# Another hand-written order for the opening's steps, with fewer and smaller filler products, and alternating state buffers

## The chip, the cores and the metric

The kernel runs on one core of one Trainium2 chip. The metric is the device time of one execution in microseconds (us). TensorE does the matrix products (PE in the profile, its weight loads PEld), VectorE is DVE, ScalarE is ACT, GpSimd is POOL, and SyncE (SP) issues nearly all loads.

## The reference

A recurrent attention with a decaying state feeds a gated feed-forward layer. There are 4 batches, 8 heads, 768 time steps and heads of 48; the layer has 3072 tokens, 384 inputs and 1536 hidden units, all float32.

```python
for t in range(S):
    cur = np.einsum('bhd,bhe->bhde', u[None] * kt, vt)
    y[:, :, t] = np.einsum('bhd,bhde->bhe', rt, state + cur)
    state = wt[:, :, :, None] * state + np.einsum('bhd,bhe->bhde', kt, vt)
...
gate = 1.0 / (1.0 + np.exp(-(x @ w_gate)))
val = x @ w_val
return (gate * val @ w_out).astype(np.float32)
```

## The kernel before

Time is cut into six chunks of 128 steps. A chunk of one batch is a block q (24 of them, four to a chunk, numbered chunk by chunk). The hidden units are cut into 12 slices f of 128, each with its own weights. The opening covers the blocks 0 to 11 and prepares 12 and 13. It runs the layer for the blocks 0 and 1 (group 0), 2 and 3 (group 1) and 4 to 7 (group 2), while the weights are still being loaded and split. After it a regular loop takes chunk after chunk; that loop is the same in both kernels.

The opening is not scheduled by a compiler. `ORDER` is a text of some 620 words; each word is one step, and the steps are issued exactly in that order. Every engine takes its own instructions in the order in which they were issued, so a word's place decides what it stands behind on each engine that it uses. The queue of SP is such an order too. Semaphores hold back an instruction whose input is not there, and everything behind it on its engine waits along.

The words that the text below uses, with q the block, g the group, f the slice:

- `pinq`, `tokq`, `wordsf`: loads on SP (decay, k and r of a block, L341; its r, v, k by token, L346; the raw weights of a slice, L279). `pin` and `tok` have two buffers each, so a load waits for the last reader of the block two before it.
- `pkq`: DVE scan of the decays (L396), a reciprocal (L400) and k times the decays (L402). `prq`: the second scan (L413) and r times it (L418). `fadeq`: the state times the chunk's decay (L408).
- `tkq`: PE transposes k (L428); `kTq`: ACT copies it out (L432). `guardq`: ACT sums squares for a bounds check (L423).
- `ssq`: PE scores and state sums (L447, L550). `m0q`, `m1q`: DVE masks the scores (L538). `midq`, `keepq`: the state at mid-chunk (ACT L559 for q below 4, else DVE L561) and at the end (DVE L565). `sxq`: PE products of state, scores and values (L461, L574).
- `b1_q` to `b4_q`: the bonus term (POOL L366, L369, DVE L373, POOL L386 and L387). `ybq`: PE adds it (L582); `y0q`, `y1q` take the result out (ACT L587 for q below 4, else DVE L590). `txq`: PE transposes it (L596); `xfq`, `xhq`, `xlq` copy it and split it (ACT L609, ACT L616 or L618, DVE L622).
- `wgf`, `wbf`, `wtf`: float64 weights become float32 (ACT L286, DVE L297, DVE L301). `whf`, `wlf`: their high and low parts (ACT L324, DVE L327).
- `pgg_f`, `pug_f`: PE products with gate and value weights (L632 for the first few slices, in plain float32 with one product; L635 else, three products with the parts). `sg`, `hm`, `hh`, `hl`: sigmoid (ACT L646), gate times value (DVE L653), its high part (ACT L660), its low part (DVE L664). `dng_f`: PE products with the output weights (L675 plain, L679 in three parts).
- `first`, `st256`, `st512`: PE products of constants, 256 or 512 columns wide (L741). Nothing reads their result; the text calls them unread products.

The functions that the diff touches beside the table:

Of the kernel before, what the change touches and what calls it, by code (L numbers as in the profile page):

```python
# [37 lines left out]
ORDER = """
first pin0 pk0 pin1 pr0 tk0 st512 tok0 kT0 ub guard0 pk1 tok1 ss0 st256 words4 pr1 tk1 st512 m00 b1_1 m10 kT1 words0 b1_0 mid0
ss1 keep0 b2_0 wg4 b2_1 b3_0 words1 sx0 st512 st512 mid1 wb4 b4_0 b3_1 wg0 wt4 yb0 pin2 b4_1 m01 m11 keep1 y00 wb0 wh4 sx1 wt0  # L40
guard1 yb1 wl4 words5 y10 tx0 y01 y11 wb1 wg1 tx1 st512 pk2 xf1 xf0 pin3 pg0_0 pr2 tok2 tk2 sg0_0 pu0_0 wt1 guard2 tok3 kT2 pk3
pg0_1 words2 ss2 sg0_1 b1_2 hm0_0 pu0_1 mid2 m02 b2_2 wg5 keep2 words3 b1_3 b3_2 dn0_0 m12 pr3 tk3 sx2 words6 kT3 wg2 b2_3 hm0_1
ss3 xh0 wb2 b4_2 b3_3 dn0_1 pin4 mid3 m03 guard3 keep3 b4_3 m13 wg3 sx3 wt2 tok4 wb3 yb2 words7 wb5 pg0_2 y02 wt3 xh1 wh2 pu0_2
wt5 sg0_2 pin5 pk4 pg0_3 wh5 yb3 tok5 hm0_2 tk4 xl1 y03 pu0_3 y13 pr4 kT4 sg0_3 dn0_2 xl0 fade4 hm0_3 pg0_4 guard4 wl5 pu0_4
sg0_4 pk5 wg6 ss4 y12 wg7 tx2 wb6 tx3 pg0_5 mid4 b1_5 keep4 hm0_4 m04 dn0_3 b2_5 sg0_5 m14 xf2 xf3 pr5 wh1 pu0_5 tk5 sx4 b1_4
kT5 xh2 wt6 ss5 pin6 b2_4 hm0_5 wh6 pg1_0 m05 fade5 hh0_4 wl6 wh3 pu1_0 words8 sg1_0 hl0_4 hh0_5 xl2 dn0_4 wb7 m15 pg0_6 hm1_0
b3_4 wl2 pu0_6 sg0_6 guard5 pg1_1 b4_4 hm0_6 mid5 hh0_6 hl0_5 xh3 keep5 wh0 pu1_1 y04 hl0_6 b3_5 sg1_1 y14 b4_5 dn0_5 hm1_1 xl3
sx5 pk6 words9 tx4 pg1_2 y05 wt7 dn1_0 sg1_2 wl1 wh7 tok8 dn1_1 wl3 tok6 pu1_2 pr6 pg1_3 words10 hm1_2 dn0_6 sg1_3 wl7 xh4 wg8
pu1_3 xl4 b1_6 pin7 y15 hh1_2 pg0_7 hm1_3 b2_6 hh1_3 tx5 tk6 wb8 xh5 pu0_7 sg0_7 xl5 hl1_2 pg1_4 hm0_7 wt8 pu1_4 sg1_4 kT6 wl0
wh8 dn1_2 wg9 hm1_4 words11 ss6 hl1_3 wl8 hh0_7 dn1_3 hh1_4 hl0_7 m06 pg1_5 fade6 b3_6 mid6 b4_6 pu1_5 keep6 sg1_5 guard6 pg0_8  # L50
hm1_5 wb9 dn0_7 wt9 sg0_8 hh1_5 pu0_8 m16 hl1_4 hl1_5 pg1_6 pk7 sx6 sg1_6 wg10 hm0_8 pr7 dn1_4 wh9 tok7 pu1_6 wl9 dn1_5 pin11
hm1_6 pg1_7 hh1_6 hl1_6 wb10 pu1_7 sg1_7 y06 b1_7 y16 pg1_8 hm1_7 b2_7 tx6 sg1_8 tk7 hh0_8 pu1_8 hh1_7 xh6 hl1_7 wg11 hl0_8
dn1_6 hm1_8 fade7 xl6 guard7 dn1_7 wt10 kT7 pg1_9 hh1_8 b3_7 pk11 pu1_9 sg1_9 wh10 ss7 b4_7 hm1_9 pg0_9 m07 mid7 m17 keep7 dn0_8
pr11 sg0_9 hh1_9 sx7 wl10 pu0_9 pin8 fade11 hl1_8 guard11 pg1_10 hl1_9 hm0_9 wb11 pu1_10 sg1_10 wt11 hh0_9 tok11 dn1_8 hl0_9
wh11 y07 dn1_9 hm1_10 y17 wl11 pg0_10 pu0_10 b1_11 tx7 tk11 xh7 b1_8 dn0_9 sg0_10 hh1_10 hm0_10 b2_11 pg0_11 hh0_10 hl1_10
pu0_11 b2_8 sg0_11 kT11 pg1_11 hl0_10 hm0_11 pk8 hh0_11 pu1_11 sg1_11 dn0_10 xl7 hm1_11 dn1_10 fade8 hh1_11 hl0_11 hl1_11 ss11
dn0_11 mid11 pr8 dn1_11 pg2_0 m011 guard8 b3_8 m111 b4_8 out1_2 b3_11 keep11 b4_11 pu2_0 sg2_0 out0_0 out1_3 tk8 sx11 kT8 ss8
pin9 y011 hm2_0 hh2_0 pg2_1 m08 mid8 out0_1 y111 hl2_0 dn2_0 sg2_1 pk9 pu2_1 pg2_2 hm2_1 keep8 hh2_1 hl2_1 pu2_2 pr9 sg2_2 m18
dn2_1 hm2_2 hh2_2 hl2_2 sx8 fade9 dn2_2 tok9 pg2_3 pin10 pu2_3 sg2_3 guard9 pg2_4 hm2_3 y08 hh2_3 hl2_3 pu2_4 pk10 sg2_4 dn2_3
y18 fade10 hm2_4 hh2_4 hl2_4 tx8 tk9 pr10 pg2_5 kT9 xh8 xl8 b1_9 dn2_4 sg2_5 b2_9 ss9 pu2_5 pg2_6 hm2_5 mid9 keep9 m09 b3_9  # L60
pu2_6 m19 sg2_6 b4_9 hh2_5 hl2_5 sx9 dn2_5 y09 pin12 hm2_6 y19 hh2_6 hl2_6 tk10 tx9 kT10 pg2_7 tok10 pu2_7 sg2_7 xh9 guard10 xl9
b1_10 dn2_6 hm2_7 b2_10 hh2_7 ss10 pg2_8 mid10 m010 hl2_7 m110 pk12 dn2_7 sg2_8 pu2_8 pg2_9 hm2_8 hh2_8 hl2_8 pu2_9 b3_10 sg2_9
keep10 b4_10 sx10 hm2_9 hh2_9 dn2_8 y010 pin13 hl2_9 fade12 pr12 dn2_9 y110 tok13 guard12 pg2_10 tok12 pu2_10 sg2_10 pg2_11
hm2_10 hh2_10 hl2_10 pu2_11 sg2_11 dn2_10 hm2_11 hh2_11 hl2_11 tx10 tx11 dn2_11 xh10 b1_12 xh11 xl11 b2_12 xl10 b3_12 ahead
out2_1 b4_12 out2_3 out2_0 out2_2
"""
# [145 lines left out]
def tile_kernel(ctx: ExitStack, tc: tile.TileContext, dec: bass.AP, tok: bass.AP, wts: bass.AP, u: bass.AP, out: bass.AP):  # L212
# [341 lines left out]

    def middle(q):

        mid[q] = mids[q % 2]
        if q < B:
            nc.scalar.copy(by_pair(mid[q]), bank["v", q, 0])  # L559
# [333 lines left out]
```

## Time and profile before

| | |
|---|---|
| median of 3 runs | 558.78 us (558.17 to 559.55) |
| profiled execution, its own time | 559.54 us |
| its span, first to last instruction | 557.8 us |
| PE busy | 543.8 us, 97% |
| DVE busy | 333.6 us, 60% |
| ACT busy | 254.2 us, 46% |
| POOL busy | 108.8 us, 20% |
| opening, up to the first product of the loop (`ahead`) | about 221 us |

The profiled execution took 0.76 us more than the median. Its time contains its span and 1.7 us around it. Times in the text are counted from the span's start. A row of the timeline has a start, the length that its instructions cover, engine, line, operation, what it writes and reads, the count, and in brackets the engine's idle time ahead of it with what ended it. Ends of matrix products are modelled, so neighbouring rows overlap a little and a short wait can hide in a row that looks busy.

### The profile page before, as it was taken

What the parts mean: (1) busy time and instruction counts of PE and PEld (TensorE: products, weight loads), DVE (VectorE), ACT (ScalarE), POOL (GpSimd) and SP (SyncE); (2) the same over time, 40 slices, a digit from 0 to 9 for tenths busy, and PEclk for the clock granted to TensorE, in tenths of its full rate; (3) what the DMA queues carried; (4) which work ended last, traced back from release to release, by engine and by line L of the source; (5) the groups of instructions that cost most, each with busy time, mean ns of one, the idle gap of its engine ahead of it and who ended that gap; (6) DMA issues with size and microseconds to landing.
All of it is one profiled execution on the core that took longest, in us unless ns stands there. A gap on an engine that the chain in (4) does not pass through costs nothing.

```text
span 557.8 us, 13756 instructions
## 1 busy us (share of the span) xinstructions
PE 543.8 (97%) x5875; PEld 455.5 (82%) x5875; DVE 333.6 (60%) x550; ACT 254.2 (46%) x598; POOL 108.8 (20%) x104
## 2 busy tenths in 40 slices
...
GB/s 292 417 386 198 144 311 87 101 101 43 115 58 1 102 139 62 116 133 141 89 147 147 113 163 162 61 164 161 116 165 120 102 65 60 63 0 2 0 1 59
DMA packets 20658, 68.46 MB, mean 123 GB/s; under 512 B 3057, under 2 KB 6769, under 8 KB 19057
## 3 DMA queue, kind: packets, MB, share of 16 engines
...
q14 instruction: 19, 0.15, 0.1%
...
## 4 chain that ended last, share of the span: by engine, by line
PE 87%; DVE 5%; ACT 3%; DMA 2%; issue 1%; POOL 1%; SPq 1%; ACTq 0%; DVEq 0%; POOLq 0%
PE pg L635 24%; PE pu L635 24%; PE po L700 17%; PE po L679 7%; PE pt L484 2%; PE pa L447 2%; DMA tok<-tok 2%; PE pa L550 2%; PE po L675 1%; PE pk L428 1%; PE pa L574 1%; PE pu L632 1%; PE pa L461 1%; PE pg L632 1%; PE px L596 1%
## 5 line engine op out<-in xcount | busy, mean ns | idle before, releaser
L635 PE MATMUL pg<-x,w 128*128 128x512 f32 (+1 forms) x702 | 156.3, 367 | 0.9 <-ACT sq L317 0.7
L635 PE MATMUL pu<-x,w 128*128 128x512 f32 (+1 forms) x702 | 155.6, 366 | 0.0
L635 PEld LDWEIGHTS pg<-x,w 128*128 128x128 f32 x702 | 121.6, 188 | 23.1 <-ACT sq L317 1.1
L635 PEld LDWEIGHTS pu<-x,w 128*128 128x128 f32 x702 | 122.1, 188 | 21.7
L653 DVE TENSOR_TENSOR sg<-pu,sg 128x512 f32<-128x512 f32 (+1 forms) x84 | 51.5, 613 | 139.0 <-PE pu L635 133.4
L646 ACT ACTIVATE sg<-pg 128x512 f32<-128x512 f32 (+1 forms) x84 | 45.2, 538 | 129.5 <-PE pg L635 120.8
L660 ACT CAST hh<-sg 128x512 fp32r<-128x512 f32 (+1 forms) x75 | 42.6, 570 | 106.1 <-DVE sg L653 106.1
L700 PE MATMUL po<-hh,w 128*128 128x512 f32 x288 | 88.7, 390 | 0.0
L366 POOL TENSOR_TENSOR bon<-tok,ub 128x384 f32<-128x384 f32 x24 | 33.2, 1386 | 242.1 <-DMA tok<-tok 168.1
L664 DVE TENSOR_TENSOR hl<-sg,hh 128x512 fp32r<-128x512 f32 (+1 forms) x78 | 51.9, 671 | 41.1 <-ACT hh L660 38.7
L700 PEld LDWEIGHTS po<-hh,w 128*128 128x128 f32 x288 | 54.1, 188 | 11.0
L700 PE MATMUL po<-hl,w 128*128 128x512 f32 x144 | 57.4, 399 | 0.0
L679 PE MATMUL po<-w,hh 128*128 128x384 f32 x168 | 42.9, 336 | 0.0
L396 DVE TENSOR_TENSOR_SCAN eg<-pin,ends 112x516 f32<-112x516 f32 x24 | 33.7, 1405 | 6.2 <-DMA pin<-dec 4.3
L369 POOL TENSOR_TENSOR bon<-bon,tok 128x384 f32<-128x384 f32 x24 | 32.0, 1337 | 1.6
L700 PEld LDWEIGHTS po<-hl,w 128*128 128x128 f32 x144 | 27.0, 188 | 6.1 <-DVE hl L664 0.2
L381 POOL TENSOR_TENSOR at<-same,a 128x512 f32<-128x512 bf16 x12 | 22.2, 1851 | 44.4 <-DVE a L373 44.4
L679 PEld LDWEIGHTS po<-w,hh 128*128 128x128 f32 x168 | 30.5, 188 | 0.3
L413 DVE TENSOR_TENSOR_SCAN eg<-pin,heads 112x516 f32<-112x516 f32 x24 | 30.3, 1263 | 0.0
L423 ACT ACTIVATE junk<-eg 112x1032 bf16<-112x1032 f32 x24 | 25.5, 1061 | 8.5 <-DVE eg L413 8.5
L679 PE MATMUL po<-w,hl 128*128 128x384 f32 x84 | 29.3, 349 | 0.0
L418 DVE TENSOR_TENSOR pin<-pin,eg 112x512 f32<-112x512 f32 x24 | 25.5, 1062 | 0.8
(111 smaller groups left out, 621.2 us busy)
## 6 DMA issues: line engine op xcount, KB each, us to landing
...
wraw<-wts SPq DMA_DIRECT2D x12, 1151.6 KB, 10.5
...
```

Source lines behind the costliest of these rows:

```text
L366: nc.gpsimd.tensor_tensor(out=bon[q][:, :DM], in0=tk[q][:, 0:DM], in1=ub, op=ALU.mult)
L369: nc.gpsimd.tensor_tensor(out=bon[q][:, :DM], in0=bon[q][:, :DM], in1=tk[q][:, 2 * DM:], op=ALU.mult)
L396: nc.vector.tensor_tensor_scan(out=e[:, 516:0:-1], data0=t[:, 516:0:-1], data1=ends[:, 516:0:-1], initial=0.0, op0=ALU.mult, op1=ALU.add,)
L413: nc.vector.tensor_tensor_scan(out=e[:, WW:WW + 516], data0=t[:, 0:516], data1=heads[:, 0:516], initial=0.0, op0=ALU.mult, op1=ALU.add,)
L418: nc.vector.tensor_tensor(out=rr(q), in0=rr(q), in1=er, op=ALU.mult)
L635: nc.tensor.matmul(t, lhsT=w[f][:, cols], rhs=x[n][:, a, k, i0 * C:i1 * C], start=k == 0 and j == 0, stop=k == NKT - 1 and j == 2)
L646: nc.scalar.activation(sg, hid["g", n, f, i0], AF.Sigmoid)
L653: nc.vector.tensor_tensor(out=sg, in0=hid["u", n, f, i0], in1=sg, op=ALU.mult)
L660: nc.scalar.copy(hh, hid["s", n, f, i0])
L664: nc.vector.tensor_tensor(out=hl, in0=hid["s", n, f, i0], in1=hid["hi", n, f, i0].bitcast(F32), op=ALU.subtract)
L679: nc.tensor.matmul(po[n, i][:, :DM], lhsT=h[:, c], rhs=w[f][:, 2 * DM:], start=f == 0 and j == 0, stop=f == NFF - 1 and j == 2,)
L700: nc.tensor.matmul(po[n, k], lhsT=w[f][:, cols], rhs=h, start=f == 0 and j == 0, stop=f == NFF - 1 and j == 2)
```

## The change

The words of `ORDER` stand in another order from the tenth on. Of the unread products, one of 256 and five of 512 columns become three of 256 and two of 512, in other gaps. The two buffers of `ready` and of `mid` are no longer taken by the parity of the block, but in turn of use (block 11 comes ahead of 8, 9 and 10, so parity gave the same buffer to 7 and 11).

```diff
@@ ORDER (its first lines)
-first pin0 pk0 pin1 pr0 tk0 st512 tok0 kT0 ub guard0 pk1 tok1 ss0 st256 words4 pr1 tk1 st512 m00 b1_1 m10 kT1 words0 b1_0 mid0
-ss1 keep0 b2_0 wg4 b2_1 b3_0 words1 sx0 st512 st512 mid1 wb4 b4_0 b3_1 wg0 wt4 yb0 pin2 b4_1 m01 m11 keep1 y00 wb0 wh4 sx1 wt0
...
+first pin0 pk0 pin1 pr0 tk0 st512 tok1 kT0 tok0 guard0 pk1 ub words4 pr1 ss0 mid0 tk1 st256 m00 b1_1 m10 kT1 words0 keep0 b1_0
+ss1 b2_1 sx0 st512 mid1 wg4 b2_0 b3_1 words1 guard1 b4_1 b3_0 m01 b4_0 m11 keep1 wg0 sx1 wb0 pin2 wb4 wt4 yb1 yb0 st256 tok2 wg1
...
     def fade(q):
 
-        ready[q] = readies[q % 2]
+        ready[q] = readies[len(ready) % 2]
...
     def middle(q):
 
-        mid[q] = mids[q % 2]
+        mid[q] = mids[len(mid) % 2]
```

What this moves, at three places. First DVE, from `wt1` (the last step that makes slice 1's weights) on; the number in a name is the block's or slice's, the one behind the underscore is the program's own. Before:

```order
L301 SCALAR_TENSOR_TENSOR spare11_330<-wraw1_265,spare11_330 128x1152
L396 SCALAR_TENSOR_TENSOR eg3_432<-pin3_404,ends_77 112x516
L400 RECIPROCAL heads_80<-eg3_432 112x4
L402 TENSOR_TENSOR pin3_404<-pin3_404,eg3_432 112x512
L653 TENSOR_TENSOR sg0_0_0_419<-pu0_0_0_421,sg0_0_0_419 128x256
L538 TENSOR_TENSOR at2_442<-pa2_0_443,after_82 128x256
L565 TENSOR_TENSOR state2_106<-pa2_1_444,mid0_108 112x192
L373 TENSOR_REDUCE a02_495<-bon2_479 128x8
L538 TENSOR_TENSOR at2_442<-pa2_1_444,after_82 128x256
L413 SCALAR_TENSOR_TENSOR eg3_432<-pin3_404,heads_80 112x516
L418 TENSOR_TENSOR pin3_404<-pin3_404,eg3_432 112x512
```

And now:

```order
L301 SCALAR_TENSOR_TENSOR spare11_360<-wraw1_306,spare11_360 128x1152
L396 SCALAR_TENSOR_TENSOR eg3_458<-pin3_378,ends_77 112x516
L400 RECIPROCAL heads_80<-eg3_458 112x4
L402 TENSOR_TENSOR pin3_378<-pin3_378,eg3_458 112x512
L413 SCALAR_TENSOR_TENSOR eg3_458<-pin3_378,heads_80 112x516
L418 TENSOR_TENSOR pin3_378<-pin3_378,eg3_458 112x512
L538 TENSOR_TENSOR at2_423<-pa2_0_424,after_82 128x256
L538 TENSOR_TENSOR at2_423<-pa2_1_425,after_82 128x256
L565 TENSOR_TENSOR state2_106<-pa2_1_425,mid0_108 112x192
L653 TENSOR_TENSOR sg0_0_0_469<-pu0_0_0_462,sg0_0_0_469 128x256
L297 TENSOR_SCALAR spare10_571<-wraw2_396 128x1152
```

`pr3` has moved ahead of `hm0_0`, the masks and the state of block 2 and `b3_2`. `wl4`, which stood before `wb1`, now stands some ten steps behind `pr3`.

Second the queue of SP, from the weights of slice 1 on. Before:

```order
L279 DMA wraw1_265<-wts 128x9213
L341 DMA pin2_322<-dec 128x1544
L279 DMA wraw5_380<-wts 128x9213
L341 DMA pin3_404<-dec 128x1544
L346 DMA tok2_412<-tok 128x1152
L346 DMA tok3_428<-tok 128x1152
L279 DMA wraw2_440<-wts 128x9213
L279 DMA wraw3_491<-wts 128x9213
```

And now:

```order
L279 DMA wraw1_306<-wts 128x9213
L341 DMA pin2_362<-dec 128x1544
L346 DMA tok2_373<-tok 128x1152
L341 DMA pin3_378<-dec 128x1544
L279 DMA wraw2_396<-wts 128x9213
L346 DMA tok3_419<-tok 128x1152
L279 DMA wraw3_467<-wts 128x9213
L279 DMA wraw5_484<-wts 128x9213
```

The raw weights of slice 5 went behind five other loads.

Third DVE again, ahead of `wl7`, the low part of slice 7's weights, which `pg0_7` needs. Before:

```order
L327 TENSOR_TENSOR w1_821<-spare11_330,w1_821 128x1152
L327 TENSOR_TENSOR w3_942<-spare10_593,w3_942 128x1152
L413 SCALAR_TENSOR_TENSOR eg6_1080<-pin6_927,heads_80 112x516
L418 TENSOR_TENSOR pin6_927<-pin6_927,eg6_1080 112x512
L653 TENSOR_TENSOR sg0_2_2_1106<-pu0_2_2_1118,sg0_2_2_1106 128x256
L327 TENSOR_TENSOR w7_1109<-full7_963,w7_1109 128x1152
```

And now:

```order
L301 SCALAR_TENSOR_TENSOR full7_994<-wraw7_692,full7_994 128x1152
L664 TENSOR_TENSOR hl0_2_2_1018<-sg0_2_2_977,hh0_2_2_996 128x256
L396 SCALAR_TENSOR_TENSOR eg6_1022<-pin6_951,ends_77 112x516
L400 RECIPROCAL heads_80<-eg6_1022 112x4
L402 TENSOR_TENSOR pin6_951<-pin6_951,eg6_1022 112x512
L327 TENSOR_TENSOR w7_1020<-full7_994,w7_1020 128x1152
```

`wl1` and `pr6` no longer stand ahead of `wl7`; `wl1` comes 13 us of DVE work later, since only group 2 needs it.

More of the change, by code (lines that the diff above doesn't have):

```diff
@@ L38 @@
 ORDER = """
-first pin0 pk0 pin1 pr0 tk0 st512 tok0 kT0 ub guard0 pk1 tok1 ss0 st256 words4 pr1 tk1 st512 m00 b1_1 m10 kT1 words0 b1_0 mid0
-ss1 keep0 b2_0 wg4 b2_1 b3_0 words1 sx0 st512 st512 mid1 wb4 b4_0 b3_1 wg0 wt4 yb0 pin2 b4_1 m01 m11 keep1 y00 wb0 wh4 sx1 wt0
-guard1 yb1 wl4 words5 y10 tx0 y01 y11 wb1 wg1 tx1 st512 pk2 xf1 xf0 pin3 pg0_0 pr2 tok2 tk2 sg0_0 pu0_0 wt1 guard2 tok3 kT2 pk3
-pg0_1 words2 ss2 sg0_1 b1_2 hm0_0 pu0_1 mid2 m02 b2_2 wg5 keep2 words3 b1_3 b3_2 dn0_0 m12 pr3 tk3 sx2 words6 kT3 wg2 b2_3 hm0_1
@@ L43 @@
[L43 to L62, printed above, removed]
@@ L63 @@
-keep10 b4_10 sx10 hm2_9 hh2_9 dn2_8 y010 pin13 hl2_9 fade12 pr12 dn2_9 y110 tok13 guard12 pg2_10 tok12 pu2_10 sg2_10 pg2_11
-hm2_10 hh2_10 hl2_10 pu2_11 sg2_11 dn2_10 hm2_11 hh2_11 hl2_11 tx10 tx11 dn2_11 xh10 b1_12 xh11 xl11 b2_12 xl10 b3_12 ahead
-out2_1 b4_12 out2_3 out2_0 out2_2
+first pin0 pk0 pin1 pr0 tk0 st512 tok1 kT0 tok0 guard0 pk1 ub words4 pr1 ss0 mid0 tk1 st256 m00 b1_1 m10 kT1 words0 keep0 b1_0
+ss1 b2_1 sx0 st512 mid1 wg4 b2_0 b3_1 words1 guard1 b4_1 b3_0 m01 b4_0 m11 keep1 wg0 sx1 wb0 pin2 wb4 wt4 yb1 yb0 st256 tok2 wg1
@@ new lines @@
+wt0 y00 pin3 y10 wb1 tx0 st256 pk2 xf0 y01 y11 words2 xh0 tx1 xf1 pr2 tk2 pg0_0 kT2 wt1 tok3 guard2 ss2 pk3 pu0_0 mid2 words3
+sg0_0 pr3 tk3 pg0_1 kT3 words5 wg2 m02 b1_3 ss3 m12 keep2 hm0_0 b1_2 wg3 sx2 wb2 sg0_1 wh4 pu0_1 b2_3 m03 pin4 guard3 wt2 dn0_0
+mid3 xh1 b2_2 hm0_1 b3_3 pg0_2 words6 wl4 pu0_2 sg0_2 b3_2 b4_3 keep3 dn0_1 xl1 b4_2 m13 hm0_2 sx3 wb3 tok4 wt3 yb2 xl0 wh3
+pg0_3 pk4 pin5 y02 wg5 pu0_3 wb5 wh2 words7 tk4 fade4 yb3 wt5 y12 sg0_3 tx2 pg0_4 pr4 wh5 tok5 dn0_2 b1_4 hm0_3 guard4 words8
@@ new lines @@
+pu0_4 wl5 y03 xf2 dn0_3 kT4 sg0_4 b2_4 hm0_4 pg0_5 hh0_4 wh0 pk5 pu0_5 y13 sg0_5 ss4 hl0_4 wb6 tx3 wl0 tk5 xf3 dn0_4 b1_5 hm0_5
+b3_4 pg1_0 hh0_5 wg6 mid4 hl0_5 m04 b2_5 pu1_0 keep4 xh3 m14 xh2 wt6 sg1_0 wg7 dn0_5 b4_4 hm1_0 pg1_1 wh6 xl3 wl3 kT5 pu1_1
+sg1_1 wl2 sx4 wl6 dn1_0 pin6 xl2 hm1_1 pr5 pg1_2 pu1_2 sg1_2 words9 y04 fade5 pg1_3 hm1_2 wb7 hh1_2 dn1_1 y14 sg1_3 wt7 guard5
+pg0_6 words10 hl1_2 wh7 pk6 ss5 wg8 dn1_2 wl7 sg0_6 tok6 pu0_6 pg0_7 hm0_6 b3_5 mid5 pu1_3 b4_5 m05 sg0_7 wh1 keep5 m15 pg1_4
@@ new lines @@
+hm1_3 pr6 hh1_3 hh0_6 sx5 sg1_4 hl0_6 pu0_7 fade6 pin7 y05 hl1_3 y15 dn0_6 hm0_7 wb8 tx4 wt8 tk6 xh4 pu1_4 guard6 tok7 b1_6
+dn1_3 wh8 hm1_4 xl4 pg1_5 hh0_7 wl8 hh1_4 pu1_5 sg1_5 hl0_7 kT6 wb9 wg9 dn0_7 hm1_5 hl1_4 wl1 pg0_8 pu0_8 pk7 sg0_8 words11 tx5
+dn1_4 xh5 hh1_5 b1_7 hm0_8 xl5 pg1_6 wt9 ss6 sg1_6 wg10 b2_6 pu1_6 m06 wh9 m16 b2_7 mid6 keep6 pg1_7 hm1_6 hh0_8 hh1_6 hl0_8
+pu1_7 pr7 sg1_7 wg11 sx6 b3_6 hl1_5 dn0_8 b4_6 hm1_7 pin11 wl9 dn1_5 pg1_8 y06 fade7 y16 wb10 tx6 tk7 b3_7 xh6 pu1_8 hl1_6 sg1_8
@@ new lines @@
+guard7 b4_7 dn1_6 hm1_8 kT7 xl6 hh1_8 pk11 pg1_9 hh1_7 pu1_9 sg1_9 hl1_8 pg0_9 wt10 ss7 sg0_9 hl1_7 wh10 hm1_9 dn1_7 mid7 hh1_9
+m07 m17 keep7 pu0_9 hl1_9 fade11 wl10 dn1_8 hm0_9 sx7 wb11 wt11 pg0_10 pin8 dn1_9 sg0_10 hh0_9 wh11 hl0_9 pu0_10 y07 tok8 pg1_10
+hm0_10 wl11 hh0_10 dn0_9 sg1_10 tok11 hl0_10 y17 pu1_10 pg0_11 hm1_10 pr11 hh1_10 dn0_10 sg0_11 pu0_11 b1_11 tk11 hl1_10 tx7
+kT11 pg1_11 b2_11 hm0_11 xh7 hh0_11 b1_8 xl7 pu1_11 sg1_11 guard11 hl0_11 dn1_10 b2_8 hm1_11 hh1_11 dn0_11 hl1_11 b3_11 pk8
```

9 lines of the change are left out of this document (added).

## Prediction

> **What bounds the kernel now.** I read the page first, then windows by stage, then the waits, the chain of waits and the timelines of PE and DVE. The page's span and PE row, and the windows (length, then busy time of PE, PEld, DVE, ACT, POOL, then granted clock, DMA share, GB/s):
>
> ```profile
> span 557.8 us, 13756 instructions
> PE 543.8 (97%) x5875; PEld 455.5 (82%) x5875; DVE 333.6 (60%) x550; ACT 254.2 (46%) x598; POOL 108.8 (20%) x104
> ...
> 14.00:28.00 14.00, 11.16 (x235) 7.79 (x227) 11.92 (x18) 8.38 (x18) 7.35 (x8) 1.00 1.01 419
> 28.00:42.00 14.00, 13.22 (x323) 10.17 (x322) 13.41 (x21) 8.16 (x15) 8.49 (x8) 1.00 0.98 384
> 42.00:56.00 14.00, 13.74 (x138) 11.79 (x137) 13.79 (x23) 9.35 (x17) 1.71 (x2) 1.00 0.48 193
> ...
> 44.68:220.70 176.02, 175.53 (x2191) 158.20 (x2190) 122.03 (x210) 68.85 (x135) 33.89 (x34) 1.00 0.29 107
> ```
>
> PE is busy 97% of the span, and all useful PE work stays. What the change can move is PE's idle time and the unread products in the first 42 us, and short waits up to 221 us. The granted clock is full in all four rows. From 16 us on DVE is the engine with no room: 11.92, 13.41 and 13.79 of 14 us. The waits of PE name one large stop, and the chain says what the start of the dense stretch hangs on:
>
> ```profile
> PE pa L574 <- issue: 1.9, 1, 1.9
> ...
> 28.48 1.22 DVE spare L301
> ...
> 31.06 1.12 DVE pin L402
> ...
> 32.57 1.56 PE pu L632 x6
> ```
>
> The stop of 1.9 us, inside `sx0` (block 0's products with state and scores), has no releaser in the profile. Up to 32.57 the chain runs over DVE, step behind step; from there over PE. So the question is where DVE's new order puts the step for which PE waits last.
>
> **Front, up to `pg0_3`.** All needed rows of DVE's groups in 14 to 42 us (busy, mean ns):
>
> ```profile
> L538 DVE TENSOR_TENSOR at<-pa,after 128x256 f32<-128x256 f32 x7 | 2.8, 417 | 0.5 <-ACT mid L559 0.5
> L373 DVE TENSOR_REDUCE a<-bon 128x8 f32<-128x384 f32 x4 | 2.2, 544 | 1.9 <-POOL bon L369 1.9
> L565 DVE TENSOR_TENSOR state<-pa,mid 112x192 f32<-112x192 f32 x4 | 1.4, 349 | 0.1
> L327 DVE TENSOR_TENSOR w<-full,w 128x1152 fp32r<-128x1152 f32 x1 | 1.4, 1351 | 0.0
> L653 DVE TENSOR_TENSOR sg<-pu,sg 128x256 f32<-128x256 f32 x2 | 0.8, 411 | 0.0
> ```
>
> And of its timeline and POOL's:
>
> ```profile
> 15.30 1.96 POOL L369 TENSOR_TENSOR bon<-bon,tok 128x384 f32<-128x384 f32 x2
> ...
> 16.34 0.55 DVE L373 TENSOR_REDUCE a<-bon 128x8 f32<-128x384 f32 x1 [1.85 <-POOL bon L369]
> 16.81 1.08 DVE L297 TENSOR_SCALAR full<-wraw 128x1152 int32<-128x1152 int32 x1
> 25.90 0.66 DVE L402 TENSOR_TENSOR pin<-pin,eg 112x512 f32<-112x512 f32 x1
> 26.48 1.23 DVE L413 TENSOR_TENSOR_SCAN eg<-pin,heads 112x516 f32<-112x516 f32 x1
> 27.74 0.69 DVE L418 TENSOR_TENSOR pin<-pin,eg 112x512 f32<-112x512 f32 x1
> 30.98 1.21 DVE L402 TENSOR_TENSOR pin<-pin,eg 112x512 f32<-112x512 f32 x1
> 34.24 1.94 DVE L413 TENSOR_TENSOR_SCAN eg<-pin,heads 112x516 f32<-112x516 f32 x1
> 36.22 0.98 DVE L418 TENSOR_TENSOR pin<-pin,eg 112x512 f32<-112x512 f32 x1
> ```
>
> `pr3` ends at 37.20 (36.22 + 0.98). In the new order six steps that stood ahead of it stand behind it, and none comes in: `wl4` 1.35, `hm0_0` 0.41, two masks 0.84, `keep2` 0.35, `b3_2` 0.54, together 3.49. A row covers 0.08 more than the step to the next one (16.34 + 0.55 is 16.89, the next row starts at 16.81); six times that off, 3.0 us. DVE gains no room otherwise, since it never stops in either order: its bonus step `b3_1` now comes first at 16.34, and `b3_0` waits some 0.4 us for POOL's second product of the pair that ends at 17.26. One gain: the L402 of block 3 covers 1.21 instead of 0.66 beside POOL's work, which now comes later; take 0.5 of it. So `pr3` ends at 37.2 - 3.0 + 0.4 - 0.5 = 34.1.
>
> `ss3`, block 3's scores, needs `pr3`, and now stands ahead of `sx2`, `pu0_1`, `dn0_0`, `pg0_2`, `pu0_2`, `dn0_1`, `sx3` and `yb2`, after which comes `pg0_3`. PE reaches it earlier: `pg0_0` starts near its 26.06, and it, `ss2`, `pu0_0`, `tk3` and `pg0_1` fill some 6 us and a wait of under 1 us for block 3's L402, to about 33. So `ss3` starts at 34.1, about 1 us after PE is free. These nine steps and `tk3` filled PE from 32.57 to 44.68 before:
>
> ```profile
> 26.06 1.56 PE L632 MATMUL pg<-spare,spare 128*128 128x256 f32 x6 [0.82 <-ACT spare L609]
> 35.26 0.55 PE L428 MATMUL pk<-ident,pin 112*128 112x112 f32 x4
> 35.74 0.67 PE L461 MATMUL pa<-mid,pin 48*64 48x48 f32 x16
> 44.68 1.46 PE L632 MATMUL pg<-spare,spare 128*128 128x256 f32 x6
> ```
>
> 12.11 less `tk3` (35.26 to 35.74, 0.48) is 11.6; two waits of 0.1 in it go, so 11.4, and `pg0_3` starts at 45.5 instead of 44.68. What stands ahead of it is the same set of steps, so the front loses 0.8 us. Bounds: if all of POOL's disturbance of block 3's steps goes (0.55, and L413 and L418 at 1.23 and 0.69 instead of 1.94 and 0.98), `pr3` ends at 33.1 and the front gains 0.2; with the next PE limit at 33 it cannot gain much more, 0.4. If as much comes on top (L297 shows it too, 1.08), it ends at 35.1 and the front loses 1.8. I take the middle value, since POOL now starts on block 3's bonus just when `pr3` runs.
>
> The unread products in the gaps:
>
> ```profile
> 10.95 0.70 PE L741 MATMUL stir<-ends 112*128 112x256 f32 x2
> 12.04 1.04 PE L741 MATMUL stir<-ends 112*128 112x512 f32 x2
> ```
>
> Three of 1.04 go and two of 0.70 come, 1.7 us of PE. They stand where PE waits for ACT, POOL or DVE anyway (0.82 in the row of `pg0_0`), so I count 0; uncovered they would be worth up to 1.7, but the limit of 33 above allows none of it. The stop of 1.9 in `sx0` has the same work ahead of it but one unread product; I leave it. `sx1` waits for DVE's masks behind it in either order.
>
> The queue of SP: slice 5's raw weights go behind five loads.
>
> ```profile
> wraw<-wts SPq DMA_DIRECT2D x12, 1151.6 KB, 10.5
> ```
>
> At the 419 GB/s above that is 2.8 us earlier for those, and for slice 5 later by the time of the five. Its first DVE step moves behind `pk4`, past 45 us, and I find nothing late: 0. ACT takes slice 1's weights ahead of `y00`; that costs `pg0_0` half a microsecond, inside the wait before `ss3`. The turn of buffers frees `fade11` from block 7's readers, and DVE has room there: 0.
>
> **Middle, `pg0_3` to the loop.** PE has the same steps in another order. Before, it shows short waits for DVE:
>
> ```profile
> 47.05 0.57 PE L428 MATMUL pk<-ident,pin 112*128 112x112 f32 x4 [0.26 <-PE pa L582]
> 75.44 1.53 PE L635 MATMUL pu<-x,w 128*128 128x256 f32 x9
> 76.81 1.24 PE L635 MATMUL pg<-x,w 128*128 128x256 f32 x9
> 78.94 1.23 PE L635 MATMUL pu<-x,w 128*128 128x256 f32 x9
> 80.16 1.31 PE L635 MATMUL pg<-x,w 128*128 128x256 f32 x9
> 101.97 1.24 PE L635 MATMUL pg<-x,w 128*128 128x256 f32 x9
> 103.44 0.61 PE L596 MATMUL px<-ident,bon 128*128 128x128 f32 x3 [0.23 <-DVE bon L590]
> ...
> 73.92 2.63 DVE L327 TENSOR_TENSOR w<-spare,w 128x1152 fp32r<-128x1152 f32 x2
> 78.67 1.35 DVE L327 TENSOR_TENSOR w<-full,w 128x1152 fp32r<-128x1152 f32 x1
> ```
>
> Such a block takes 1.08 (76.81 to its successor). From 75.44 to 76.81 are 1.37: PE waits 0.3 for `wl3`, which ends at 76.55. From 78.94 to 80.16 are 1.22: 0.14, for `wl7`, which ends at 80.02. From 101.97 to 103.44 are 1.47, 0.4 with the row's 0.23 in it. With the 0.26 at 47.05 that is 1.1. In the new order `wl7` has `wl1` (1.27 with overlap taken off), `pr6` (1.8) and eight short steps (2.6) no longer ahead, and `hl1_2` and `wl0` (1.6) more: it ends near 76.0. PE has `sx5` (1.4), `pu1_3` (1.2), `dn0_6` (1.0) and `tx4` (0.3) no longer ahead of `pg0_7`, and `dn1_2` (1.1) more: it gets there at 77.3, or 78.1 with the front's loss. So that wait goes, and the others likewise, -1.1. Bounds: two more hidden waits like that at 101.97 may sit in blocks that I did not take apart and go too, -1.8; the new order can bring as many waits in new places as it takes away and one more, about +1.0 on the whole.
>
> **Sum.** +0.8 - 1.1 = -0.3: 559.54 becomes 559.2. That execution was 0.76 above the median; against 558.78 the same -0.3 gives 558.5.
>
> **The rivals.**
> Faster: POOL leaves DVE alone and all waits in the middle go, -0.4 - 1.8 = -2.2, so 556.6. For it speaks that DVE's disturbed rows stand in one place (30.98 to 37.2); against it that POOL's steps have to be done in that stretch still.
>
> Slower, by DVE: `pr3` ends at 35.1 or later, +1.8, and a DVE that late keeps the waits of the middle: 560.6. It decides from `pr3` at 35.0. For it speaks that DVE has 0.2 of 14 us free in the window up to 56, so any stop of it reaches PE.
>
> Slower, by the clock: PE does less to fill its gaps between 19 and 33 us, and the granted clock, 1.00 in every window above, falls to half there. The work of that stretch, some 9 us, would take 18, less 4 of waits: +5, so 563.8. Against it: the longest stop before was 1.9 us (the waits), and none that I work out is longer. [...]
>
> **How the numbers follow.** My forecast is no change that can be told, 558.5: 0.56. Faster rival and what lies between: 0.29. DVE late: 0.12. Clock: 0.03. A measurement of this kernel tells about 0.3%, 1.7 us, from no change: so faster 0.29, same 0.56, slower 0.15. The range reaches from the faster rival, 556.6, to the late DVE, rounded down to 560.4.
>
> **What would show it.** Right: the fourth L418 on DVE ends near 34.1 and the L447 of block 3 starts behind it; the fourth `pg` block of L632 starts near 45.5; no `pg` or `px` block between 44 and 110 waits for DVE; clock 1.00. Wrong: that `pg` block starts below 44 or above 46.5, or DVE idles between 17 and 82 us, or a new PE wait above 0.5 us stands in the middle.

## The result and the profile after

| | before | after |
|---|---|---|
| median | 558.98 us (558.17 to 559.98, 5 runs) | 562.77 us (561.47 to 563.43, 5 runs) |
| profiled execution | 559.54 us | 563.11 us |
| PE resumes in `sx0` | 17.85 | 19.85 |
| `ss3` starts (nine steps fewer ahead of it in after) | 37.35 | 37.66 |
| `pg0_3` starts | 44.68 | 48.83 |
| `ahead` starts | 220.72 | 225.25 |

The kernel became slower, by a ratio of 1.0054 with a 95% interval of 1.0028 to 1.0080. The prediction said no change, 558.5 us in a range from 556.6 to 560.4. It was wrong in sign and size.

The page of after, first and PE row, then its windows by the stages of the prediction (columns as there):

```profile
span 561.4 us, 13755 instructions
PE 544.2 (97%) x5873; PEld 457.0 (81%) x5873; DVE 330.5 (59%) x550; ACT 253.1 (45%) x598; POOL 107.6 (19%) x104
```

```profile
14.00:28.00 14.00, 9.93 (x220) 7.71 (x212) 11.54 (x18) 5.80 (x8) 5.54 (x8) 0.76 0.92 358
28.00:42.00 14.00, 11.88 (x248) 9.23 (x247) 10.29 (x14) 9.88 (x21) 6.16 (x4) 1.00 0.74 298
42.00:56.00 14.00, 13.36 (x140) 10.49 (x138) 13.25 (x21) 7.35 (x14) 6.24 (x6) 1.00 0.86 309
48.83:225.25 176.42, 175.78 (x2191) 158.17 (x2191) 121.32 (x211) 70.08 (x138) 38.28 (x36) 1.00 0.31 113
```

PE's total hardly moved (543.8 to 544.2), so neither the page's shares nor the count of instructions shows the loss. The windows do: from 14 to 28 the granted clock is 0.76 instead of 1.00, and from 28 to 42 PE is busy 11.88 instead of 13.22, because DVE (10.29 instead of 13.41) got its work late. All of the loss is there by `pg0_3`: 48.83 less 44.68 is 4.15. From there on the two are nearly equal: up to `ahead` after takes 0.38 more (176.42 instead of 176.04), and from `ahead` to the end 0.93 less (336.15 instead of 337.08), in one execution of each. So the two spans differ by 3.6.

The waits of PE in after, and its timeline (start, length, what, idle time ahead of it in brackets):

```profile
PE pa L574 <- issue: 4.1, 1, 4.1
...
PE pu L635 <- DVE sg L653: 0.6, 1, 0.6
```

```profile
14.98 0.79 PE L574 MATMUL pa<-tok,at 64*32 64x48 f32 x55
19.85 0.31 PE L574 MATMUL pa<-tok,at 64*32 64x48 f32 x9 [4.07 <-issue]
20.09 2.07 PE L741 MATMUL stir<-ends 112*128 112x512 f32 x2
22.09 1.09 PE L461 MATMUL pa<-mid,pin 48*64 48x48 f32 x16
23.11 1.50 PE L574 MATMUL pa<-tok,at 64*32 64x48 f32 x64
...
30.28 1.56 PE L632 MATMUL pg<-spare,spare 128*128 128x256 f32 x6 [0.28 <-ACT spare L609]
...
37.66 0.69 PE L447 MATMUL pa<-pin 48*64 48x64 f32 x32 [1.39 <-DVE pin L418]
...
48.83 1.46 PE L632 MATMUL pg<-spare,spare 128*128 128x256 f32 x6
```

The stop inside `sx0` is the one that the prediction saw in before and left alone. It was 1.93 us and is 4.07. In before it comes two products earlier in `sx0`, behind 53 of the 64 instead of 55, as the same timeline of before shows:

```profile
17.85 0.36 PE L574 MATMUL pa<-tok,at 64*32 64x48 f32 x11 [1.93 <-issue]
18.14 2.31 PE L741 MATMUL stir<-ends 112*128 112x512 f32 x4
```

Behind the stop the work of after runs at half speed: a group of 64 L574 takes 1.50 there and 0.88 or 0.89 at the full clock, and the one unread product of 512 columns (two rows) takes 2.07, where two of them (four rows) took 2.31 in before.

### The profile page after: what moved, and what is told of

Read it like the earlier page. It is cut to its first block, busy times and chain, and to the rows that moved or that the text cites. A ratio compares the mean times of both kernels' runs of the same rounds, so it can differ in the third digit from the quotient of the medians.

```text
span 561.4 us, 13755 instructions
## 1 busy us (share of the span) xinstructions
PE 544.2 (97%) x5873; PEld 457.0 (81%) x5873; DVE 330.5 (59%) x550; ACT 253.1 (45%) x598; POOL 107.6 (19%) x104
## 4 chain that ended last, share of the span: by engine, by line
PE 89%; DVE 4%; ACT 3%; issue 2%; DMA 1%; ACTq 0%; SPq 0%; DVEq 0%
PE pg L635 24%; PE pu L635 24%; PE po L700 16%; PE po L679 8%; PE pa L447 2%; PE pt L484 2%; PE pa L574 2%; PE pa L550 2%; PE stir L741 1%; PE pk L428 1%; PE pa L461 1%; PE pu L632 1%; PE po L675 1%; DMA x<-gap 1%; DVE eg L413 1%
## 5 line engine op out<-in xcount | busy, mean ns | idle before, releaser
L366 POOL TENSOR_TENSOR bon<-tok,ub 128x384 f32<-128x384 f32 x24 | 32.0, 1336 | 237.4 <-DMA tok<-tok 151.9
L423 ACT ACTIVATE junk<-eg 112x1032 bf16<-112x1032 f32 x24 | 25.4, 1060 | 4.9 <-DVE eg L413 4.9
```

Source lines behind the costliest of these rows:

```text
L366: nc.gpsimd.tensor_tensor(out=bon[q][:, :DM], in0=tk[q][:, 0:DM], in1=ub, op=ALU.mult)
```

## The theory, and its rivals

The explanation lies in the DMA queue that the page calls "q8 instruction": 47 packets with 0.77 MB, so 16 KB each.

```profile
q8 instruction: 47, 0.77, 0.5%
```

By the packets' records in the traces the first of them in the span starts at 15.40 in before and at 17.40 in after, and in both PE resumes 2.45 us later (17.85 and 19.85). There is one packet to 252 of PE's records (11,837 records over 47 packets in before, 11,826 over 47 in after). I read this as PE waiting in `sx0` for its own instructions; the wait's row names no releaser but "issue".

What releases that packet I took from a count. I counted PE's records (products, weight loads and the few of its sequencer) up to each point. In the eleven kernels of this study that stop in `sx0`, the stop lies between the 449th and the 450th record, whatever the time; before stops two products earlier in `sx0` because it has four records more ahead. In all but e7 the packet's service begins 3.0 to 4.0 us after PE has started about its 180th record. Before has 181 records ahead of `ss1`; the 180th belongs to the unread product `st512` in the gap ahead of it and starts at 12.05. After has one unread product less there, so 177 records ahead of `ss1` (the expectation of e5 has 183 and 179; the four between them are what matters). Its 180th belongs to `ss1` itself, which waits for DVE until 13.46. The theory: **an unread product of 1 us (1.04 at 12.04 in before) also carries PE's count of instructions past the point at which the next ones are asked for, while PE would wait anyway. Without it the request leaves 1.4 us later, and the small products behind it are used up in 2.3 us (13.46 to 15.78).** The rest of the 2.0 us is the packet's own delay, 3.93 instead of 3.35 us. Behind the longer stop the granted clock falls (0.50 from 20.00 to 26.83 in after; 1.00 from 14 to 28 in before). That there is a request, and that it leaves near the 180th record, is inferred from these times; no record shows the request itself.

The stop's length also hangs on when PE runs out: `ss1` starts at 13.46 in some profiles and at 14.07 in others. Where the request leaves ahead of `ss1`, as in before, a later `ss1` makes the stop shorter by as much (e10: `ss1` 0.61 later than in before, stop 1.31 instead of 1.93). The time at which PE goes on is the cleaner measure.

The rivals were the order in which the first loads stand on SP (`tok1` ahead of `tok0` and `ub`), DVE being late by itself, and the unread products behind the stop.

## The experiments

| run | PE stop in `sx0` | half clock in the profile, from 14 us on | median us (runs) | ratio to before, 95% |
|---|---|---|---|---|
| after | 4.1 | 20.0 to 26.8 | 562.77 (5) | 1.0054 [1.0028, 1.0080] |
| e1, after, loads as before | 3.1 | 15.7 to 25.9 | 563.71 (10) | 1.0066 [1.0043, 1.0089] |
| e2, after, two `st512` ahead of `sx0` | none | 12.6 to 16.0, 26.2 to 29.6 | 559.28 (10) | 0.9994 [0.9973, 1.0016] |
| e3, before, loads as after | 1.3 | none | 559.46 (10) | 0.9996 [0.9972, 1.0021] |
| e4, after, three `st512` behind `sx0` | 3.4 | 20.8 to 24.2 | 565.76 (4) | 1.0124 [1.0080, 1.0168] |
| e5, after, `st256` cut in two | 2.1 | 19.9 to 26.7 | 563.04 (8) | 1.0061 [1.0032, 1.0090] |
| e6, before less one `st256` | 4.0 | 20.6 to 27.4 | 563.20 (8) | 1.0055 [1.0030, 1.0081] |
| e7, after, 60 small products first | none (1.2 later, in `sx2`) | none | 572.66 (1) | no interval |
| e8, before, its two `st512` ahead of `sx0` | none | none | 559.35 (10) | 0.9995 [0.9979, 1.0012] |
| e9, e5 and a second `st512` behind | 2.7 | 18.6 to 25.4 | 565.44 (4) | 1.0107 [1.0053, 1.0162] |
| e10, before, one `st512` behind | 1.3 | none | 560.24 (10) | 0.9994 [0.9966, 1.0022] |
| e11, e2 and `hm0_3` ahead of `pr4` | 1.3 | none | 559.02 (10) | 0.9992 [0.9965, 1.0018] |
| e12, e11 with wider unread products | 0.8 | none | 559.36 (10) | 0.9999 [0.9971, 1.0027] |

**The loads, e1 and e3.** e1 puts the order of the first loads of before into after, e3 that of after into before.

```diff
e1 -tk0 st512 tok1 kT0 tok0 guard0 pk1 ub words4 pr1 ss0
   +tk0 st512 tok0 kT0 ub guard0 pk1 tok1 words4 pr1 ss0
e3 -tk0 st512 tok0 kT0 ub guard0 pk1 tok1 ss0 st256
   +tk0 st512 tok1 kT0 tok0 guard0 pk1 ub ss0 st256
```

> The changed kernel with one thing put back: the first loads stand as before (block 0's tokens, u, block 1's tokens; the change had block 1's, block 0's, u). Theory F (the stop of TensorE inside sx0, 4.07 us after the change against 1.93 before, is a late load of its instructions, and the clock falls because of that stop): if the order of these loads is what made the load late, the stop returns to about 1.9, the clock stays at 1.00, and the time is 558.5 to 560. If the load's delay has another source, 4 us and 562.8 remain. Theory S (fewer unread products let the clock fall): 562.8, the clock falls as before. Theory O (the new order makes ACT and DVE late: y00 behind the weights, the bounds check of block 2 ahead of block 3's scan): 562 to 563 whatever the clock does.

> The kernel before with one part of the change alone: the first loads in the changed order (block 1's tokens, block 0's, u). Theory F with the loads' order as the source: the stop in sx0 grows from 1.9 to about 4 us, the clock falls to half for one to three windows of 3.4 us, and the time rises to 561 to 563. Theory F with another source, S and O: nothing but noise, 558.5 to 559.5.

e1 stays as slow as after, e3 as fast as before. The loads' order is not the source. PE goes on at 20.15 in e1 (19.85 in after) and at 17.83 in e3 (17.85 in before); e3's stop is the shorter one because its `ss1` starts at 14.07. In e1's profile the clock fell at 15.70, ahead of the stop, behind 1.59 us of idle time in front of `ss1`, so that profile does not show a fall caused by the stop.

**Unread products ahead of or behind the stop, e2 and e4.**

```diff
e2 -ss1 b2_1 sx0 st512 mid1
   +ss1 b2_1 st512 st512 sx0 mid1
e4 +ss1 b2_1 sx0 st512 st512 st512 mid1
```

> The changed kernel with the 512-column unread product that stood behind sx0 doubled and put ahead of sx0, behind ss1. TensorE then has about 1.8 us of work between the point where it asks for instructions and the point where it lacks them. Theory F: the stop in sx0 shrinks from 4.1 to about 2.3 us, too short for the clock to fall; the granted clock is 1.00 in 20 to 27 us, and the time is 558.5 to 560. Theory S: there is one product of 512 columns more, so the clock may hold too, but the stop stays at 4. Theory O: 562 to 563.

> The changed kernel with three instead of one 512-column unread products behind sx0, so that it has as many as the kernel before had columns in that stretch and more. Theory S: the clock stays at 1.00 and the time falls to 559 to 560. Theory F: the products stand behind the stop, so the stop stays at about 4 us, the clock falls as in the changed kernel, and at half pace the products themselves take 1.7 us each: 562.8 to 565. Theory O: 562.8 to 564.

e2 shows it from the side of after: the same work plus one unread product, and the loss is gone. Its timeline of PE has no gap in `sx0`, and `pg0_3` starts where it did in before:

```profile
15.41 2.58 PE L741 MATMUL stir<-ends 112*128 112x512 f32 x4
...
18.51 1.06 PE L574 MATMUL pa<-tok,at 64*32 64x48 f32 x64
...
44.63 1.48 PE L632 MATMUL pg<-spare,spare 128*128 128x256 f32 x6
```

By the theory the products fill the time in which the instructions are on their way. In this execution the clock was half from 12.6 to 16.0, so `ss1` (0.91 to the next row instead of 0.52 in after) and the first of these products took longer and covered more (the two took 2.51, 15.41 to 17.92, and 2.25 in e11); e11 and e12, with the same two products, still stopped for 1.3 and 0.8 and were as fast. That a stop of 2.3 would be too short for the clock to fall was my estimate, between 1.9 in before and 4.1 in after; e5's 2.1 was long enough. In e4 the same kind of product stands behind the stop. There it hides nothing of the stop (3.4) and runs for the greater part at half speed (three products in 5.01, 19.37 to 24.38), and by the medians the kernel loses 3.0 us more than after.

**The count alone, e5 and e6.** e5 cuts one unread product of after into two of half the width: four records more ahead of `ss1` (181, as in before), with the same columns. e6 takes one unread product out of before and leaves 177, as in after.

```diff
e5 -ss0 mid0 tk1 st256 m00      (after)
   +ss0 mid0 tk1 st128 st128 m00
e6 -tok1 ss0 st256 words4       (before)
   +tok1 ss0 words4
```

> The changed kernel with the 256-column unread product between tk1 and ss1 cut into two of 128 columns: as many columns, four TensorE records more ahead of ss1 (183 as before the change, not 179). Theory P: TensorE asks for its next 256 instructions when it passes a fixed place in its list, which lies behind the 179th and not behind the 183rd record; before the change it passed it at 12.05 us with the unread product ahead of ss1, after it only when ss1 starts at 13.46. From passing to the end of the stop are 5.8 us before. So here it passes at 12.5, the load is served near 15.9 instead of 17.4, the stop in sx0 is about 2.9 instead of 4.1 us, the clock falls in part of the runs only, and the time is 559.5 to 561.5. Theory S (columns of unread products hold the clock) and theory O (ACT and DVE order): 562.8, stop 4.1.

> The kernel before without its 256-column unread product between ss0 and tk1; the one of 512 columns ahead of ss1 stays. Four records fewer, 179 instead of 183, as after the change. Theory P: the place is passed only when ss1 starts, the load is served near 17, the stop grows from 1.9 to about 3.5 to 4 us, the clock falls in nearly all runs, and the time is 561 to 563. Theory S: 256 of 2816 columns and no new gap over 1 us, no change, 559. Theory O: no change, 559.

The 256 of e5's expectation is a distance that e7's stops show below (256 and 768 records behind the place in `sx0`); that PE asks for its instructions at a fixed place is the theory, and no run shows the asking.

The first waits of PE in e5 and in e6:

```profile
PE pa L574 <- issue: 2.1, 1, 2.1
```

```profile
PE pa L574 <- issue: 4.0, 1, 4.0
```

Both stops went where the count says, in both directions: from 4.1 to 2.1 and from 1.9 to 4.0. In e5 0.6 of the 1.9 is not the count's, since `ss1` starts 0.6 later than in after (14.07) and PE runs out later. The other 1.3 is: the 180th record starts at 12.59, the packet at 16.07, and PE goes on at 18.53 instead of 19.85. e9 below has the same cut with `ss1` at 13.46, and its stop is 2.7. e6 shows it from the side of before: one unread product less, PE goes on at 20.51 instead of 17.85, and the kernel has the whole loss, 1.0055 beside 1.0054. But e5's time did not follow its stop. All eight runs had a mean clock of 0.994 or less, and the median is that of after. In this order a stop of 2 us was enough to lose the clock (2.15 in the profile, then 0.50 from 19.91 to 26.73).

**Starting with small products, e7.** It was to carry the count past the point while PE is still waiting for its first data. It fills the start with 60 products of 64 columns instead of four of the nine wide ones.

```diff
-[stir(blank[:, :P], blank[:, :512]) for _ in range(9)]
+[stir(blank[:, :32], blank[:, :64]) for _ in range(60)] + [stir(blank[:, :P], blank[:, :512]) for _ in range(5)]
```

> The changed kernel with the nine first unread products of 512 columns replaced by 60 of 64 columns and 32 rows of result and five of 512 columns: some 112 records more ahead of the first transposition, in time in which TensorE has nothing else. Theory P: the place is passed in ss0's scores near 9.7 us, the load is there by 15.5, the stop in sx0 shrinks below 1 us, the clock stays at 1.00 in 14 to 28 us, and one look gives 558 to 560. Theory S and O: 4 us and 561 to 563. [...]

The timeline of PE in e7:

```profile
1.38 19.17 PE L741 MATMUL stir<-blank 128*32 128x64 bf16 x65 [1.38 <-DVE blank L268]
20.34 0.95 PE L428 MATMUL pk<-ident,pin 112*128 112x112 f32 x4
```

The row covers 65 products in 19.17 us; nine wide ones took 5.73 in after. The first transposition starts at 20.34 instead of 6.91, so the time says nothing on the question. It was my mistake to price a product by its columns: one after another into the same bank, these took about 0.27 us each (19.17 less five of 0.64, over 60). What sets that price was not tried.

The count it does bear out. PE has no stop in `sx0` and waits on "issue" twice later, in `sx1` and `sx2`:

```profile
31.86 0.44 PE L574 MATMUL pa<-tok,at 64*32 64x48 f32 x19 [0.27 <-issue]
47.76 0.38 PE L574 MATMUL pa<-tok,at 64*32 64x48 f32 x17 [1.20 <-issue]
```

These stops lie between the 705th and 706th and between the 1217th and 1218th record, 256 and 768 behind the place in the other kernels. So the place goes by PE's records, not by the step. And here the first packet's service begins at 23.39, only 0.7 us after the 180th record. Between the two the DMA engines moved nothing (share 0.00), where in the other thirteen profiles they were full (0.99 to 1.02). That fits a packet that waits among the loads; it is one execution, and no run tried it alone.

**The same cover in before, e8.**

```diff
-ss1 keep0 b2_0 wg4 b2_1 b3_0 words1 sx0 st512 st512 mid1
+ss1 st512 st512 keep0 b2_0 wg4 b2_1 b3_0 words1 sx0 mid1
```

> The kernel before with its two unread products of 512 columns moved from behind sx0 to ahead of it, behind ss1: the load of instructions runs while they do. Theory P: the stop of 1.9 us shrinks below 0.5, sx0 ends no later, no run has the clock fall behind it, and the time is 557.5 to 559 against 559.4, mostly because the runs at 561 to 563 go. Theory S: same columns, no change. Theory O: no change.

The stop goes and the median stays. PE runs through `sx0` and then waits for POOL, as its timeline in e8 shows:

```profile
14.52 2.31 PE L741 MATMUL stir<-ends 112*128 112x512 f32 x4
...
17.36 0.89 PE L574 MATMUL pa<-tok,at 64*32 64x48 f32 x64
19.89 0.92 PE L582 MATMUL pa<-bon,ident 128*128 128x192 f32 x4 [1.64 <-POOL bon L387]
```

What changes is the spread. Of 71 executions of before that ran beside the experiments, 27 had a mean clock under 0.9965, and the medians of these were 561.4 to 562.2 in three groups, while the others had 558.8 to 559.1. So before suffers the same fall in about four of ten executions. In e8 all ten lie between 558.55 and 560.15, two of them with a clock under 0.9965. The executions of before that lost time left no trace; that theirs is the same fall is read from clock and time alone.

**What stands behind the stop, e9 and e10.** Before has two unread products of 512 behind `sx0`, after only one. If these held the clock up, e9 should be as fast as before, and e10 slower.

```diff
e9  (e5) -sx0 st512 mid1
         +sx0 st512 st512 mid1
e10 (before) -sx0 st512 st512 mid1
             +sx0 st512 mid1
```

> The kernel after with two edits: the unread product of 256 columns between tk1 and ss1 cut into two of 128 (as in e5, where the stop in sx0 was 2.1), and a second unread product of 512 behind sx0, so that as many stand behind the stop as in the kernel before. Theory A (a stop of about 2 us does no harm if full-size products follow it for 2 us): stop 1.9 to 2.3, no half clock in the profile, 559.0 to 560.5 us. Theory B (any stop of 2 us or more in this place brings the half clock, whatever follows): half clock for 3 to 7 us behind the stop, 562.5 to 564 us, and the second product adds 0.5 more. ss3 starts by A at 33.5 to 34.5, by B at 36 to 37.5.

> The kernel before with one unread product of 512 behind sx0 instead of two; the count of instructions ahead of ss1 stays, so the stop should stay at 1.9 (1.7 to 2.1). Theory A (full-size products behind the stop hold the clock up): the half clock comes in most executions, median 561 to 563 us. Theory B (the length of the stop alone decides): no more executions at the half clock than in the kernel before (about a third), median 558.8 to 559.6 us.

The waits of PE in e9, then in e10:

```profile
PE pa L574 <- issue: 2.7, 1, 2.7
```

```profile
PE pa L574 <- issue: 1.3, 1, 1.3
```

In e9 PE goes on at 18.47 (18.53 in e5), the clock fell all the same (0.993 or less in the mean of all four runs), and with the second product the kernel took 2.4 us more than e5 (565.44 less 563.04), about what one such product takes at half clock (2.07 above). The theory that work behind the stop holds the clock falls. In e10 the stop was to stay at 1.9; it is 1.3, with `ss1` at 14.07, and PE goes on at 17.84 as in before. Seven of ten runs had a mean clock under 0.9965, more than in before, but the ratio of 0.9994 tells no difference; this one is not settled.

**A better order, e11 and e12.** e11 adds to e2 that `hm0_3` stands ahead of `pr4` on DVE. e12 also makes the two unread products behind `yb0` and `tx0` 512 wide.

```diff
e11 -pg0_4 pr4 wh5 tok5 dn0_2 b1_4 hm0_3
    +pg0_4 wh5 tok5 dn0_2 b1_4 hm0_3 pr4
e12 -yb0 st256 tok2 ... tx0 st256 pk2
    +yb0 st512 tok2 ... tx0 st512 pk2
```

> e2 (two unread products of 512 ahead of sx0, none behind, in the kernel after) with one more edit: hm0_3, the product on VectorE that reads the one bank of pu, stands ahead of pr4 instead of behind it. By the theory that pu0_4 waited for hm0_3 behind pr4's 2.6 us: the wait row of pu0_4 on hm0_3 (0.6 per execution in the kernel after) goes, dn0_2 to pu0_4 comes back to 1.0 to 1.3 us from 2.1, and the time is 558.2 to 558.9 us against 559.28 for e2. By the rival (the middle is bound by VectorE, whose work is the same, so that pr4 is late instead and its transposition tk5 waits): 559.1 to 559.8 us.

> e11 with the two unread products of 256 columns behind yb0 and tx0 made 512 wide. In e2 the profile showed the half clock once more from 26.2 to 29.6, with PE idle for 0.45 and 0.70 us ahead of tx1 and tk2. If thin work there lets the clock fall, the wider products hold it: no half clock after 16 us, and 0.5 to 1.5 us less than e11. If the clock there does not hang on them: the same as e11 within 0.5, or up to 0.5 more where they outlast the wait.

The wait of `pu0_4`, and what became of it. First DVE and PE in after, then PE in e11:

```profile
53.00 1.22 DVE L413 TENSOR_TENSOR_SCAN eg<-pin,heads 112x516 f32<-112x516 f32 x1
54.26 1.31 DVE L418 TENSOR_TENSOR pin<-pin,eg 112x512 f32<-112x512 f32 x1
55.50 0.41 DVE L653 TENSOR_TENSOR sg<-pu,sg 128x256 f32<-128x256 f32 x1
```

```profile
53.87 1.46 PE L675 MATMUL po<-spare,sg 128*128 128x384 f32 x4
55.96 1.34 PE L635 MATMUL pu<-x,w 128*128 128x256 f32 x9 [0.64 <-DVE sg L653]
```

```profile
49.84 1.46 PE L675 MATMUL po<-spare,sg 128*128 128x384 f32 x4
50.83 1.53 PE L635 MATMUL pu<-x,w 128*128 128x256 f32 x9
52.20 1.46 PE L675 MATMUL po<-spare,sg 128*128 128x384 f32 x4
54.04 1.31 PE L635 MATMUL pg<-x,w 128*128 128x256 f32 x9 [0.39 <-DVE w L327]
```

In after, `dn0_2` to `pu0_4` takes 2.09 (53.87 to 55.96), in e11 0.99. Of the 1.10 gained, 0.85 is given back three steps later: `dn0_3` to `pg0_5` takes 1.84 (52.20 to 54.04) instead of 0.99 in e2, since `wl5` now ends behind `pr4`. So the wait was real, and moving it shows DVE without room. Both expectations were half right, and the time cannot be told from e2's or before's. e12 has no half clock in its profile after 14.5 us, as expected, but e11 has none either, so the wider products are not shown to have done it, and there is no gain in the median. Neither version can be told from the kernel before.

## Why the clock fell

The clock's records, but for the last of a trace, last whole multiples of 3.41 us (10.24, 6.83 and 532.48 in after, 546.13 in before), and the edges of this grid lie at other times in each run (20.00 in after, 17.19 in before, 16.49 in e5). So I took windows along the grid of each run (PE busy is the first number behind the length, the granted clock the third from the end). After, before, e5, e11:

```profile
16.59:20.00 3.41, 0.15 (x9) 0.15 (x8) 3.00 (x7) 2.65 (x4) 2.94 (x5) 1.00 1.00 415
20.00:23.41 3.41, 3.41 (x43) 1.74 (x39) 3.31 (x4) 1.28 (x1) 0.00 (x0) 0.50 0.86 320
23.41:26.83 3.42, 3.42 (x69) 3.30 (x60) 3.35 (x6) 0.00 (x0) 0.00 (x0) 0.50 0.81 267
```

```profile
13.77:17.19 3.42, 2.15 (x129) 1.93 (x121) 1.52 (x4) 1.77 (x3) 3.34 (x4) 1.00 1.01 420
17.19:20.60 3.41, 2.69 (x17) 1.31 (x17) 3.41 (x7) 1.29 (x1) 3.41 (x5) 1.00 0.99 419
```

```profile
16.49:19.91 3.42, 1.38 (x15) 0.56 (x14) 3.05 (x6) 2.59 (x4) 2.19 (x5) 1.00 0.98 410
19.91:23.32 3.41, 3.41 (x84) 3.20 (x84) 3.31 (x5) 1.32 (x1) 0.00 (x0) 0.50 1.02 400
```

```profile
16.82:20.23 3.41, 2.10 (x82) 1.36 (x80) 3.29 (x7) 2.23 (x3) 2.38 (x4) 1.00 0.95 357
```

After idles for nearly the whole window and then has half the clock for two of them. Before's stop of 1.93 lies across an edge, 1.27 in one window and the rest in the next, and the clock stays. In e5 one window holds the stop, 2.04 idle of 3.42, and the clock falls. In the openings of the thirteen profiles other than e7's, a window at full clock with 1.85 us or more of idle time was followed by the half clock in each of five cases (after, e4, e5, e6, e9); from 1.15 to 1.59 idle both happened; with less it never fell. That reading fits that before falls in some executions only, as the edge comes to lie. It was read from the traces and not tried by a run of its own, and where exactly between 1.15 and 1.85 it turns, and whether thin work counts as idle, stays open. The stop's length alone does not say how often the clock falls: a mean clock under 0.9965 came in eight of eight runs of e5 (stop 2.1 in its profile), in seven of ten of e10 and four of ten of e3 (1.3), and in 27 of 71 of before (1.9).

How the loss divides, from one profile each: e5's `pg0_3` starts at 46.96, e2's at 44.63, after's at 48.83. Between e2 and e5 lie the half clock and a stop of 2.1, together 2.3 us; between e5 and after lies the rest of the stop, 1.9. The medians of e5 and after do not show that second part (563.04 and 562.77), so this split is an estimate. The sum, 4.2, is what the front lost. The half clock does not cost that much everywhere: e2's profile has it twice, from 12.6 to 16.0 and from 26.2 to 29.6, and `pg0_3` starts no later than in before.

## Why the prediction was wrong, point by point

**The stop in `sx0`: the step that failed.** "The stop of 1.9 in `sx0` has the same work ahead of it but one unread product; I leave it." The row named no releaser, and I took its length as given. That one product decided it: e6 takes one away from before and gets 563.20. It should have been asked what a wait with the name "issue" hangs on; the queue of instructions and its 16 KB packets are in the page. The eleven kernels that stop there lose 0.8 (e12) to 4.1 us (after) of PE's time by it.

**The unread products at 0.** They "stand where PE waits anyway" is true of their time and false of their effect. e2 against after: one more product, and moving two ahead of the stop, is worth 3.5 us.

**The front, +0.8.** The steps from `ss3` on were right and the input was not; "it never stops in either order", said of DVE, failed. `ss3` to `pg0_3` was put at 11.4 and takes 11.17 in after (37.66 to 48.83). `pr3` was to end at 34.1 and ends at 37.6, because PE, half as fast, kept ACT's steps back (`pg0_0` starts at 30.28 instead of 26.06) and DVE stood idle ahead of `pk3` for ACT's `guard2`. `pr3`'s own two rows took 2.02 and 1.32 besides, instead of 1.22 and 0.69 in e2. DVE in after:

```profile
31.73 1.23 DVE L396 TENSOR_TENSOR_SCAN eg<-pin,ends 112x516 f32<-112x516 f32 x1 [3.11 <-ACT junk L423]
```

With the stop covered, in e2, DVE is even a little ahead of the early bound (33.1), with rows that are not stretched:

```profile
30.76 1.22 DVE L413 TENSOR_TENSOR_SCAN eg<-pin,heads 112x516 f32<-112x516 f32 x1
32.02 0.69 DVE L418 TENSOR_TENSOR pin<-pin,eg 112x512 f32<-112x512 f32 x1
```

So `pr3` ends at 32.7, and `pg0_3` starts at 44.63, 0.05 earlier than before. So without the stop the middle value would have been too high by 0.85, inside the bounds. In after the front lost 4.15, far outside them, by the stop and the clock behind it.

**The middle, -1.1.** Mis-sized. It measured 176.42 instead of 176.04, so +0.4. The waits named did go, for instance `wl7`'s at `pg0_7`, on PE in after:

```profile
80.65 1.23 PE L635 MATMUL pu<-x,w 128*128 128x256 f32 x9
81.71 1.24 PE L635 MATMUL pg<-x,w 128*128 128x256 f32 x9
82.79 1.24 PE L635 MATMUL pu<-x,w 128*128 128x256 f32 x9
```

These starts lie 1.06 and 1.08 apart. But `pu0_4` waits 1.1 for `hm0_3`, which reads the one bank of `pu` and now stands behind `pr4`; I had not followed that bank. That is 1.1 of new wait against 1.1 gone; where the remaining 0.4 lies was not found. The prediction's bound, as many new waits as go and one more, +1.0, contained it.

**SP, ACT and buffers at 0.** e1 and e3 bear out the first loads. Slice 5's weights, ACT's `wg1` and the turn of buffers were not tried by themselves. No wait in after names the first or the last. A wait of PE for ACT's L587 of 0.4 us is new, about the half microsecond that the prediction allowed for ACT.

**The rivals.** "Slower, by the clock" at 563.8 was the outcome in kind and size (562.77) and had a chance of 0.03. The case against it, that no stop is longer than 1.9, was the failed step again; before's rows show only that the clock outlasted 1.9 us in that execution, and in e5 it did not outlast 2.1. "Slower, by DVE" saw `pr3` late, past its 35.0, though as an effect and not a cause. "Faster" did not come in any version: e2, e11 and e12, with the stop covered or short, are within 0.1% of before. For what it treated, the order of the steps, the prediction's small sum of -0.3 was right in that the new order is worth nothing that can be measured.
